# Quarter-array steps whose row halves add into the same two banks, with a drain of TensorE between

## The chip, the cores and the metric

The kernel runs on one core of a Trainium2 chip. The metric is the device time of one execution in microseconds. A core has five engines that this text names as the profile does: PE (TensorE, the matmul array, with its weight loads listed apart as PEld), DVE (VectorE), ACT (ScalarE), POOL (GpSimd) and SP (SyncE, which here only issues transfers). Matmul results go to eight PSUM banks of 128 partitions by 512 float32; only PE writes them, DVE and ACT read them out.

## The reference

Sigmoid attention on 8 batches of 12 heads, then a token mixer whose mixing matrix is made from the data:

```python
scores = q @ k.T / sqrt(64) - log(448)         # per batch and head, 448 x 448
x = (sigmoid(scores) @ v)                      # heads side by side: 8 x 448 x 768
wq, wk = x @ w_q, x @ w_k                      # 8 x 448 x 64 each
mixed = (wq @ wk.T / sqrt(64)) @ x             # 8 x 448 x 768
out = relu(mixed) @ w_out                      # 8 x 448 x 768, float32
```

The kernel computes `mixed` as `wq @ (wk.T @ x)`.

## The kernel before

**Units.** There are 24 quads: quad n = 3u + j holds four heads of batch u (j = 0, 1, 2). A head's 448 tokens are 7 blocks of 64. Everything on PE is bf16, and most of it runs in quarters of the array: a matmul of 64 rows by 64 columns of weights. Four such matmuls, one for each pair of row half and column half, run side by side; this text calls them a group. The column half decides which 64 partitions of a bank are written. The two row halves hold different parts of a sum or different operands, and they write different banks, so most steps take a pair of banks.

**Steps.** The order of the work is written out by hand in the string `PLAN`, one letter for each step; all engines' queues follow from it, and each engine works strictly in that order. The letters that matter here:

- S: scores of one block, four matmuls of 448 columns into a pair of banks, then one sigmoid on ACT (L303), which writes bf16. There are 168.
- P: sigmoid times v for one block, four matmuls of 448 columns, summed over seven steps; then the result `xt` is copied out of the banks by DVE (L329), or in halves by DVE and ACT (L327, letter R).
- x: transposes of `xt` to `xn`.
- W: `x @ [w_q w_k]` of batch u in six steps c = 0 to 5, one for each 128 columns of x. For u = 4, 5, 6 (letters L and l) the steps are tiled in quarters, step c takes `xt` of quad c // 2, and the two row halves sum into a bank each (L383). After step 5 one bank is copied to `wpart` (L390), the other is added to that on DVE (L391) and makes `wqk`; POOL copies half of it to `wq2` (L392).
- N: `wk` is transposed.
- U: `wk.T @ x` of batch u, here called `tmp`. For u = 3, 5, 6, 7 (letters T and t) it is tiled the same way, with 14 matmuls of 384 columns (L439), a copy of one bank to `upart` (L443) and an addition (L444).
- M: `wq @ tmp` with its relu (L448 on ACT, L450 on DVE), three steps for each batch.
- O: the output product. Batches 2 to 5 use whole sums per bank (`out_pair`, L509). Of the last two batches, three chunks of 128 tokens (letters I and i, `out_halves`, L549) are tiled in quarters: four parts, two for each block of 64 tokens. After the second part of a block, one bank is copied to the output tile `o` (L554) and the other added to it on DVE (L555). The other chunks run on the whole array, in halves of 384 output columns (`out_chunk`, L590, copies L614). The very last half is summed in one bank, and DVE copies 192 of its columns and ACT the other 192 (L611, L612).

**Banks.** The string `BANKS` lists by hand which bank or pair each step takes, in order of `PLAN`. A step's first matmul waits for the last reader of the bank.

**Loads.** SP issues the loads of q, k, v in the order of `ORDER`, at most eight tiles ahead of the casts to bf16. The two weights w_q and w_k are two transfers into one tile (L624); POOL casts that tile in four pieces (L720). v is cast to a tile ordered by block, then head pair (L202).

**The end.** After the last S come, in `PLAN`, the rest of batches 6 and 7: `x`, W of batch 7 on the whole array, N, U, M, twelve I steps, and sixteen O steps.

Of the kernel before, what the change touches and what calls it, by code (L numbers as in the profile page):

```python
# [17 lines left out]
def kernel(  # L18
# [29 lines left out]
    def pool(name, bufs, **kw):  # L48
# [30 lines left out]
    )  # L79
# [45 lines left out]
    def xt(u, j):  # L125
# [61 lines left out]
    def cast1(n, nm, e):  # L187
        if KIND[n] in "cer" and nm != "v":
            if n not in pq:
                pq[n] = p_c16.tile([P, 2, 2, NI, 32, 2], BF16, tag="qk16", name="qk16")  # L190
            f = pq[n]
            COPY[e](  # L192
                out=f[:, :, "qk".index(nm)].rearrange("p e i d y -> p e y i d"),
                in_=ld.pop((nm, n)).rearrange("p (y i e d) -> p e y i d", y=2, i=NI, e=2),
            )
            ld[nm + "16", n] = f
            if ("q16", n) in ld and ("k16", n) in ld:
                arrange(n, nc.gpsimd)
            return
        p = p_v16 if nm == "v" else p_c16  # L200
        t16 = p.tile([P, NI, 2, HD], BF16, tag=nm + "16", name=nm + "16")
# [111 lines left out]
    def values(n, i, tail, eng):  # L313
# [4 lines left out]
        for h in range(2):  # L318
            for g in range(2):
                nc.tensor.matmul(  # L320
                    ps[HALF[g], h, 0:S], ld["v16", n][HALF[h], i, g, :],
                    ats[n, i][HALF[h], g, :], start=(i == 0), stop=(i == NI - 1),
                )
# [52 lines left out]
    def mlp_wqk(u, c, tail, act, tiled):  # L376
        if c == 0:
            pw[u] = bank2() if tiled else bank1()
        fb, ps, _ = pw[u]
        if tiled:  # L380
            for y in range(2):
                for x in range(2):
                    nc.tensor.matmul(  # L383
                        ps[HALF[x], y, 0:S], wqk16[HALF[y], c, 64 * x : 64 * x + 64],
                        xt(u, c // 2)[HALF[y], c % 2, 0:S], start=(c == 0), stop=(c == NC - 1),
                    )
            if c == NC - 1:
                w, w2 = wqks[u % 2], wq2s[u % 2]
                part = p_one.tile([P, S], F32, tag="wpart", name="wpart")
                read(fb, COPY["s" if act else "v"](out=part, in_=ps[:, 0, 0:S]))  # L390
                read(fb, nc.vector.tensor_tensor(out=w[:, 0:S], in0=ps[:, 1, 0:S], in1=part, op=ALU.add))  # L391
                nc.gpsimd.tensor_copy(out=w2[HALF[1]], in_=w[HALF[0], 0:S])  # L392
            return
# [4 lines left out]
        if c == NC - 1:  # L398
            w, w2 = wqks[u % 2], wq2s[u % 2]
            read(fb, nc.vector.tensor_copy(out=w[:, 0:S], in_=ps))  # L400
# [29 lines left out]
    def mlp_tmp_tiled(u, act):  # L430
        tmps[u] = p_one.tile([P, NB], BF16, tag="tmp", name="tmp")
        part = p_one.tile([P, NB], F32, tag="upart", name="upart")
        fb, ps, _ = bank2()
        for m in range(4):
            for r in range(2):
                if 2 * m + r == NI:
                    continue
                for y in range(2):
                    nc.tensor.matmul(  # L439
                        ps[HALF[y], r, 0:NB], wkn[u][HALF[r], m, :], xns[u][HALF[r], m, y * NB : (y + 1) * NB],  # L440
                        start=(m == 0), stop=(m == 3 - r),
                    )
        read(fb, COPY["s" if act else "v"](out=part, in_=ps[:, 0, 0:NB]))  # L443
        read(fb, nc.vector.tensor_tensor(out=tmps[u], in0=ps[:, 1, 0:NB], in1=part, op=ALU.add))  # L444

# [85 lines left out]

    def out_halves(act):

        if opened:
            w, m, part, fb, ps = opened.pop()
        else:
            w, m, nb = chunks.pop(0)
            assert nb < 0
            part = 0
            ot[0] = p_o.tile([P, 2, NB], F32, tag="o", name="o")  # L540
        o = ot[0]
        b, h = divmod(part, 2)
        if not h:
            fb, ps, _ = bank2()
        for c in range(3 * h, 3 * h + 3):
            t0 = 2 * S * c + m * P + b * NP
            for y in range(2):
                for x in range(2):
                    nc.tensor.matmul(  # L549
                        ps[HALF[x], y, 0:NB], mxs[w][HALF[y], t0 : t0 + NP], wout16[HALF[y], c, x * NB : (x + 1) * NB],  # L550
                        start=(c == 0), stop=(c == NC - 1),
                    )
        if h:
            read(fb, COPY["s" if act else "v"](out=o[:, b], in_=ps[:, 0, 0:NB]), keep=True)  # L554
            read(fb, nc.vector.tensor_tensor(out=o[:, b], in0=ps[:, 1, 0:NB], in1=o[:, b], op=ALU.add), keep=True)  # L555
        if part < 3:
            opened.append((w, m, part + 1, fb, ps))
            return
        (b0, i0), (b1, i1) = divmod(2 * m, NI), divmod(2 * m + 1, NI)
        for x in range(2):  # L560
# [11 lines left out]
    def out_chunk(act, tail):  # L572
# [22 lines left out]
        def store(cols):  # L595
            for y in range(2):
# [5 lines left out]
                )  # L602

        ps = ps[:, 0:NB] if not part else ps
# [4 lines left out]
        if w == NU // 2 - 1 and not chunks:  # L609
            h = NB // 2  # L610
            read(fb, nc.vector.tensor_copy(out=o[:, NB : NB + h], in_=ps[:, 0:h]), keep=True)  # L611
            read(fb, nc.scalar.copy(out=o[:, NB + h :], in_=ps[:, h:]), keep=True)  # L612
        else:
            read(fb, COPY["s" if act else "v"](out=o[:, nb * NB : (nb + 1) * NB], in_=ps), keep=True)  # L614
        split = tail and w == NU // 2 - 1 and m == NI - 1
# [5 lines left out]
    def load_weights():  # L621
        w32["qk"] = p_ld.tile([P, 2 * NI * HD], F32, tag="ld", name="w32")[:, 0:D]
        for x, w in enumerate((moe_w_q, moe_w_k)):
            nc.sync.dma_start(  # L624
                out=w32["qk"].rearrange("p (c n) -> p c n", c=NC)[:, :, 64 * x : 64 * x + 64],
                in_=w.rearrange("(c p) n -> p c n", p=P)
            )

# [48 lines left out]
    OTHERS = set(BY["s"] + BY["v"])  # L677
    ORDER = [(x[0], int(x[1:])) for x in ORDER.replace(".", "").lower().split()]
    done = dict.fromkeys("SPqkKxWNUMOCgz", 0)
# [4 lines left out]
    def pump_loads():  # L684
        while len(loaded) < len(ORDER):
            nm, n = ORDER[len(loaded)]
            if nm == "w" and n:
                loaded.add((nm, n))
# [22 lines left out]
    def cast_now(nm, n, e):  # L711
# [5 lines left out]
        else:  # L717
            for h in range(2):
                for g in range(2):
                    COPY[e](  # L720
                        out=wqk16[HALF[g], h::2],
                        in_=w32["qk"].rearrange("p (c n) -> p c n", c=NC)[HALF[h], g::2],
                    )
        cast.add((nm, n))
# [4 lines left out]
    def pump():  # L729
        while pumped[0] < len(ORDER):  # L730
            nm, n = ORDER[pumped[0]]
            if (nm, n) not in OTHERS:
                if not ready(nm, n):
                    break
                cast_now(nm, n, "g")
            pumped[0] += 1
# [31 lines left out]

    ALIKE = dict(a="q", c="q", e="q", r="q", b="k", d="k", f="k", s="k", j="k", h="k", X="x", y="x", Y="x", g="g", z="z", L="W", l="W", T="U", t="U", I="O", i="O", Q="O", G="M", R="P")
    done["q"] = done["k"] = 1  # L770
    quads_r = []

    for t in PLAN:
# [59 lines left out]
        elif kind == "O":  # L833
            if (opened or chunks)[0][0] in TW:
                out_pair(t == "o", t == "Q")
            elif t in "Ii":
                out_halves(t == "i")
            else:
# [30 lines left out]
```

## Time and profile before

| | us |
|---|---|
| timed runs | 182.22, 183.09, 185.05 (median 183.09) |
| the profiled execution | 182.05 |
| its span, first to last instruction | 180.3 |
| PE busy from 160 to 180 | 16.11 |
| ACT busy from 160 to 180 | 7.18 |

The span is what the profile shows; the execution's own time adds what lies around it. In the profile, a line such as `L298 PE MATMUL banks<-qk 64*64 64x448 bf16 x672` is a group of alike instructions: line 298 of the kernel, the engine, what it writes and reads, the part of the array (64*64 is a quarter), partitions by columns, and the count. A time line gives start, length, engine and line, and in brackets how long the engine had been idle before and what released it. Matmuls overlap: a quarter matmul of 448 columns is listed with some 0.35 us, while groups of four follow each other every 0.19 us.

### The profile page before, as it was taken

The page shows a single profiled execution, that of the slowest core. Times are in us where ns is not written, and L with a number is a line of the kernel's source. Part 1 is how long each engine was busy: PE and PEld are TensorE (multiplying, and loading weights), DVE is VectorE, ACT ScalarE, POOL GpSimd, SP SyncE. Part 2 cuts the span into 40 slices and gives each one's busy share as a digit, 9 for nine tenths or more (in the row PEclk, how much of TensorE's full clock was granted, in tenths as well). Part 3 has the DMA queues.
Part 4 walks back from the last instruction along what each step waited for, and adds up shares of the span by engine and source line. Part 5 has one row for each costly group of instructions (what it writes and reads, how often), then busy time and mean ns, then how long its engine had stood idle before and what let it go on. Part 6 is the DMA issues. An engine that isn't in the chain of part 4 may idle for free.

```text
span 180.3 us, 7970 instructions
## 1 busy us (share of the span) xinstructions
PE 169.6 (94%) x3471; PEld 112.5 (62%) x3472; DVE 142.1 (79%) x229; ACT 160.0 (89%) x212; POOL 123.4 (68%) x168
## 2 busy tenths in 40 slices
PE   7787899889999999999999999999999999999990
PEld 7333555554455445655686768778987789778560
DVE  3239599998989899889899879887999866588810
ACT  4699999999999999999999989999999899985240
POOL 1397799998998999999999999989306990000000
PEclk9999999999999999999999999999999999999998
DMA  5999999999999799989998999983946744442686
GB/s 174 356 394 387 331 382 376 288 302 364 411 340 346 181 306 292 372 285 288 313 282 285 281 374 346 316 266 96 264 118 155 226 95 107 91 91 46 157 241 175
DMA packets 24915, 47.31 MB, mean 262 GB/s; under 512 B 3888, under 2 KB 18480, under 8 KB 24880
## 3 DMA queue, kind: packets, MB, share of 16 engines
q1 hardware_dynamic: 23680, 44.84, 77.0%
q0 software_dynamic: 800, 1.18, 3.6%
q10 hardware_dynamic: 400, 0.79, 1.4%
q8 instruction: 27, 0.44, 1.0%
q14 instruction: 8, 0.07, 0.1%
HBM read 35.78 MB, written 11.01 MB: 260 GB/s over the span
## 4 chain that ended last, share of the span: by engine, by line
PE 67%; DVE 14%; DMA 9%; POOL 4%; SPq 2%; ACT 2%; issue 2%
PE banks L298 13%; PE banks L320 13%; PE banks L590 13%; PE banks L509 11%; DVE qk L232 4%; DMA k<-in_k_dram 4%; DMA v<-in_v_dram 3%; PE banks L549 3%; PE banks L395 3%; DVE xt L329 3%; POOL qk L192 3%; PE banks L358 2%; DVE qk L256 2%; DVE xn L347 1%; DMA out_dram<-o 1%
## 5 line engine op out<-in xcount | busy, mean ns | idle before, releaser
L303 ACT ACTIVATE at<-banks 128x896 bf16<-128x896 f32 x168 | 140.9, 946 | 3.6 <-PE banks L298 2.7
L298 PE MATMUL banks<-qk 64*64 64x448 bf16 x672 | 62.5, 357 | 2.5 <-DVE xt L329 1.4
L320 PE MATMUL banks<-at,v 64*64 64x448 bf16 x672 | 46.5, 350 | 0.1
L298 PEld LDWEIGHTS <-qk 64*64 64x64 bf16 x672 | 25.8, 105 | 21.1 <-issue 12.5
L509 PE MATMUL banks<-wout,mx 64*64 64x384 bf16 x672 | 36.3, 323 | 0.0
L320 PEld LDWEIGHTS <-v 64*64 64x64 bf16 x672 | 23.7, 106 | 6.9 <-issue 0.8
L509 PEld LDWEIGHTS <-mx 64*64 64x64 bf16 x672 | 23.3, 107 | 4.3
L590 PE MATMUL banks<-wout,mx 128*128 128x384 bf16 x132 | 24.8, 327 | 0.0
L192 POOL CAST qk<-q 128x896 bf16<-128x896 f32 x19 | 22.6, 1191 | 0.7 <-DMA q<-in_q_dram 0.2
L450 DVE TENSOR_SCALAR mx<-banks 128x512 bf16<-128x512 f32 (+3 forms) x24 | 21.0, 882 | 2.4 <-PE banks L477 1.6
L161 POOL COPY swap<-qk 32x448 uint32<-32x448 uint32 x28 | 15.8, 564 | 10.2 <-DVE qk L192 8.5
L192 POOL CAST qk<-k 128x896 bf16<-128x896 f32 x18 | 21.5, 1194 | 1.8 <-POOL qk L167 0.9
L329 DVE CAST xt<-banks 128x896 bf16<-128x896 f32 x19 | 20.5, 1081 | 1.4 <-PE banks L320 1.0
L202 POOL CAST v<-v 128x896 bf16<-128x896 f32 x20 | 18.4, 931 | 0.6
L590 PEld LDWEIGHTS <-mx 128*128 128x128 bf16 x132 | 11.9, 98 | 10.7 <-issue 3.9
L164 POOL COPY qk<-qk 32x448 uint32<-32x448 uint32 x28 | 16.6, 592 | 1.6
L263 DVE STREAM_TRANSPOSE qk<-qk 128x448 f32<-128x448 f32 x28 | 17.3, 630 | 0.1
L167 POOL COPY qk<-swap 32x448 uint32<-32x448 uint32 x28 | 15.8, 564 | 1.6
L232 DVE STREAM_TRANSPOSE qk<-qk 32x448 f32<-32x448 f32 x24 | 15.3, 636 | 0.6
L371 DVE COPY xn<-banks 128x1024 bf16<-128x1024 bf16 (+1 forms) x17 | 11.1, 654 | 4.6 <-PE banks L358 4.6
L614 DVE COPY o<-banks 128x384 f32<-128x384 f32 x15 | 8.2, 550 | 1.6 <-PE banks L590 0.8
L358 PEld LDWEIGHTS <-xt 64*64 64x64 bf16 x544 | 7.6, 109 | 1.9 <-issue 1.0
(87 smaller groups left out, 196.2 us busy)
## 6 DMA issues: line engine op xcount, KB each, us to landing
q<-in_q_dram SPq DMA_DIRECT2D x24, 448.0 KB, 7.0
v<-in_v_dram SPq DMA_DIRECT2D x24, 448.0 KB, 6.3
k<-in_k_dram SPq DMA_DIRECT2D x23, 448.0 KB, 7.3
out_dram<-o SPq DMA_DIRECT2D x51, 192.0 KB, 3.5
wout<-in_moe_w_out_dram POOLq DMA_DIRECT2D x2, 576.0 KB, 12.1
wout<-wout SPq DMA_DIRECT2D x12, 96.0 KB, 5.2
out_dram<-o ACTq DMA_DIRECT2D x3, 192.0 KB, 3.4
k<-in_k_dram SPq DMA_DIRECT2D x1, 256.0 KB, 5.2
```

Of the source, the lines that this page charges most:

```text
L164: eng.tensor_copy(out=w[hi, 0], in_=w[lo, 1])
L192: COPY[e](out=f[:, :, "qk".index(nm)].rearrange("p e i d y -> p e y i d"), in_=ld.pop((nm, n)).rearrange("p (y i e d) -> p e y i d", y=2, ...
L202: COPY[e](out=t16.rearrange("p i b d -> p b i d"), in_=ld.pop((nm, n)).rearrange("p b (i d) -> p b i d", i=NI),)
L232: nc.vector.transpose(out=qk[n][other : other + 32, h].rearrange("p t i n -> p (t i n)").bitcast(F32), in_=w[own : own + 32, 1 - h],)
L263: nc.vector.transpose(out=qk[n][:, t].rearrange("p t i n -> p (t i n)").bitcast(F32), in_=w)
L298: nc.tensor.matmul(sc[HALF[h], g, 0:S], qk[n][HALF[g], h, 1, i, :], qk[n][HALF[g], h, 0].rearrange("p i n -> p (i n)"), start=True, stop=True,
L303: inst = nc.scalar.activation(at, sc[:, :, 0:S], ACTF.Sigmoid, bias=attn_bias, scale=attn_scale)
L320: nc.tensor.matmul(ps[HALF[g], h, 0:S], ld["v16", n][HALF[h], i, g, :], ats[n, i][HALF[h], g, :], start=(i == 0), stop=(i == NI - 1),)
L329: read(fb, COPY[eng](out=xt(u, j)[:, :, 0:S], in_=ps[:, :, 0:S]))
L450: inst = nc.vector.tensor_scalar(dst, ps, moe_scale, 0.0, ALU.mult, ALU.max)
L509: nc.tensor.matmul(ps[HALF[x], y, 0:NB], mx[HALF[y], u, b, 64 * (i - 3 * y) : 64 * (i - 3 * y) + 64], wout16[HALF[y], slot(y, b), x * NB : ...
L590: nc.tensor.matmul(ps, mxs[w][:, 2 * S * c + m * P : 2 * S * c + (m + 1) * P], wout16[:, c, w0:w1], start=(c == 0), stop=(c == NC - 1),)
```

## The change

In the tiled W, U and I steps both row halves now add into the same two banks. The columns (for I, the two token blocks) are split in two, one half for each bank. In a first pass row half 0 writes bank 0 and row half 1 bank 1; then PE is drained (`nc.tensor.drain()`); in a second pass the row halves change banks and add to what the other has left. At the end each bank holds a full sum, and one copy of both banks replaces the copy and the addition.

- W: six steps remain, with eight matmuls of 224 columns each. Step c takes both halves of quad c % 3 in pass c // 3; the drain stands ahead of step 3.
- U: 28 matmuls of 192 columns, with one drain in the middle.
- I: four parts of a chunk of 12 matmuls of 384 columns as before, with a drain ahead of part 2; one pair of banks for the chunk instead of two, and one copy of 768 columns after part 3, on DVE (I) or ACT (i). The output tile is taken only there.
- The last output half: the two 192-column halves become separate sums in separate banks, each copied after its own six matmuls, the first by DVE, the second by ACT.
- `BANKS` is changed from batch 3 on, mostly by renaming; the letters of the last steps in `PLAN` change where the copies go.
- v is cast in one piece to a tile ordered by head pair, then block. The weights come in eight transfers (2 weights, 2 partition halves, 2 parities), and are cast in one piece.

The code also gets a way to cast v by transfer (`CASTING`, marked by a star in `ORDER`) and a letter J for split copies; no star stands in `ORDER` and no J in `PLAN`.

```diff
-        "wwwwyINIIItIiIGMiIMiIIOOOOOOOQOoOQOQOQ"
+        "wwwwyINIIItIIIGMiIMIIIOOOOOOOQOoOQOQOQ"
...
+        if nm == "v":
+            t16 = p_v16.tile([P, 2, NI, HD], BF16, tag="v16", name="v16")
...
+                COPY[e](
+                    out=t16.rearrange("p b i d -> p (b i d)"), in_=ld.pop((nm, n)).rearrange("p b x -> p (b x)"),
+                )
...
         if tiled:
-            for y in range(2):
-                for x in range(2):
-                    nc.tensor.matmul(
-                        ps[HALF[x], y, 0:S], wqk16[HALF[y], c, 64 * x : 64 * x + 64],
-                        xt(u, c // 2)[HALF[y], c % 2, 0:S], start=(c == 0), stop=(c == NC - 1),
-                    )
+            z, j = divmod(c, NJ)
+            if c == NJ:
+                nc.tensor.drain()
+            for b in (2 * j, 2 * j + 1):
+                for y in range(2):
+                    for x in range(2):
+                        nc.tensor.matmul(
+                            ps[HALF[x], y ^ z, 0 : S // 2], wqk16[HALF[y], b, 64 * x : 64 * x + 64],
+                            xt(u, j)[HALF[y], b % 2, (y ^ z) * S // 2 : (y ^ z) * S // 2 + S // 2],
+                            start=(z == b == 0), stop=(z == 1 and b == NC - 1),
+                        )
             if c == NC - 1:
-                w, w2 = wqks[u % 2], wq2s[u % 2]
-                part = p_one.tile([P, S], F32, tag="wpart", name="wpart")
-                read(fb, COPY["s" if act else "v"](out=part, in_=ps[:, 0, 0:S]))
-                read(fb, nc.vector.tensor_tensor(out=w[:, 0:S], in0=ps[:, 1, 0:S], in1=part, op=ALU.add))
-                nc.gpsimd.tensor_copy(out=w2[HALF[1]], in_=w[HALF[0], 0:S])
+                src = ps[:, :, 0 : S // 2]
+                read(fb, nc.vector.tensor_copy(out=w[:, 0:S].rearrange("p (z s) -> p z s", z=2), in_=src))
...
-        read(fb, COPY["s" if act else "v"](out=part, in_=ps[:, 0, 0:NB]))
-        read(fb, nc.vector.tensor_tensor(out=tmps[u], in0=ps[:, 1, 0:NB], in1=part, op=ALU.add))
+        h = NB // 2
+        for t in range(2):
+            if t:
+                nc.tensor.drain()
+            for m in range(4):
+                for r in range(2):
+                    if 2 * m + r == NI:
+                        continue
+                    z = r ^ t
+                    for y in range(2):
+                        nc.tensor.matmul(
+                            ps[HALF[y], z, 0:h], wkn[u][HALF[r], m, :],
+                            xns[u][HALF[r], m, y * NB + z * h : y * NB + z * h + h],
+                            start=(t == m == 0), stop=(t == 1 and m == 3 - r),
+                        )
+        read(fb, COPY["s" if act else "v"](
+            out=tmps[u].rearrange("p (z x) -> p z x", z=2), in_=ps[:, :, 0:h],
+        ))
...
-    def out_halves(act):
+    def out_halves(act, split):
...
+        z, h = divmod(part, 2)
+        if part == 2:
+            nc.tensor.drain()
         for c in range(3 * h, 3 * h + 3):
             for y in range(2):
+                t0 = 2 * S * c + m * P + (y ^ z) * NP
                 for x in range(2):
                     nc.tensor.matmul(
-                        ps[HALF[x], y, 0:NB], mxs[w][HALF[y], t0 : t0 + NP], wout16[HALF[y], c, x * NB : (x + 1) * NB],
-                        start=(c == 0), stop=(c == NC - 1),
+                        ps[HALF[x], y ^ z, 0:NB], mxs[w][HALF[y], t0 : t0 + NP],
+                        wout16[HALF[y], c, x * NB : (x + 1) * NB],
+                        start=(part == 0 and c == 0), stop=(z == 1 and c == NC - 1),
                     )
-        if h:
-            read(fb, COPY["s" if act else "v"](out=o[:, b], in_=ps[:, 0, 0:NB]), keep=True)
-            read(fb, nc.vector.tensor_tensor(out=o[:, b], in0=ps[:, 1, 0:NB], in1=o[:, b], op=ALU.add), keep=True)
...
+            read(fb, COPY["s" if act else "v"](out=o, in_=ps[:, :, 0:NB]), keep=True)
...
+        if nb and w == NU // 2 - 1 and not chunks:
+            if part:
+                fb, ps, _ = bank1()
+            h = NB // 2
+            c0 = NB + part * h
+            block(ps[:, 0:h], c0, c0 + h, 0, NC)
+            read(fb, COPY["vs"[part]](out=o[:, c0 : c0 + h], in_=ps[:, 0:h]), keep=True)
...
-            nc.sync.dma_start(
-                out=w32["qk"].rearrange("p (c n) -> p c n", c=NC)[:, :, 64 * x : 64 * x + 64],
-                in_=w.rearrange("(c p) n -> p c n", p=P)
-            )
+            for g in range(2):
+                for h in range(2):
+                    nc.sync.dma_start(
+                        out=w32["qk"][HALF[g]].rearrange("p (j h n) -> p h j n", j=NJ, h=2)[:, h, :, 64 * x : 64 * x + 64],
+                        in_=w.rearrange("(j g h d) n -> g h d j n", j=NJ, g=2, h=2)[g, h],
+                    )
...
-            for h in range(2):
-                for g in range(2):
-                    COPY[e](
-                        out=wqk16[HALF[g], h::2],
-                        in_=w32["qk"].rearrange("p (c n) -> p c n", c=NC)[HALF[h], g::2],
-                    )
+            COPY[e](out=wqk16.rearrange("p c n -> p (c n)"), in_=w32["qk"])
```

More of the change, by code (lines that the diff above doesn't have):

```diff
@@ L199, in cast1 @@
             return
-        p = p_v16 if nm == "v" else p_c16
-        t16 = p.tile([P, NI, 2, HD], BF16, tag=nm + "16", name=nm + "16")
+        if nm == "v":
+            t16 = p_v16.tile([P, 2, NI, HD], BF16, tag="v16", name="v16")
+            if e == "d":
+                u, j = quads[n]
+                nc.gpsimd.dma_start(
+                    out=t16.rearrange("p b i d -> p b (i d)"),
+                    in_=v[u, 4 * j : 4 * j + 4].rearrange("(g h) (p i) d -> (h p) g (i d)", g=2, i=NI),
+                )
+            else:
+                COPY[e](
+                    out=t16.rearrange("p b i d -> p (b i d)"), in_=ld.pop((nm, n)).rearrange("p b x -> p (b x)"),
+                )
+            ld["v16", n] = t16
+            return
+        t16 = p_c16.tile([P, NI, 2, HD], BF16, tag=nm + "16", name=nm + "16")
         COPY[e](
@@ L379, in mlp_wqk @@
         fb, ps, _ = pw[u]
+        w, w2 = wqks[u % 2], wq2s[u % 2]
         if tiled:
-            for y in range(2):
-                for x in range(2):
-                    nc.tensor.matmul(
-                        ps[HALF[x], y, 0:S], wqk16[HALF[y], c, 64 * x : 64 * x + 64],
-                        xt(u, c // 2)[HALF[y], c % 2, 0:S], start=(c == 0), stop=(c == NC - 1),
-                    )
-            if c == NC - 1:
-                w, w2 = wqks[u % 2], wq2s[u % 2]
-                part = p_one.tile([P, S], F32, tag="wpart", name="wpart")
-                read(fb, COPY["s" if act else "v"](out=part, in_=ps[:, 0, 0:S]))
-                read(fb, nc.vector.tensor_tensor(out=w[:, 0:S], in0=ps[:, 1, 0:S], in1=part, op=ALU.add))
-                nc.gpsimd.tensor_copy(out=w2[HALF[1]], in_=w[HALF[0], 0:S])
+            z, j = divmod(c, NJ)
[9 more added lines that the diff above has]
+                        )
+            if c == NC - 1:
+                src = ps[:, :, 0 : S // 2]
+                read(fb, nc.vector.tensor_copy(out=w[:, 0:S].rearrange("p (z s) -> p z s", z=2), in_=src))
+                if tail or act:
+                    read(fb, nc.scalar.copy(out=w2[HALF[1]].rearrange("p (z s) -> p z s", z=2), in_=src[HALF[0]]))
+                else:
+                    nc.gpsimd.tensor_copy(out=w2[HALF[1]], in_=w[HALF[0], 0:S])
             return
@@ L431, in mlp_tmp_tiled @@
         tmps[u] = p_one.tile([P, NB], BF16, tag="tmp", name="tmp")
-        part = p_one.tile([P, NB], F32, tag="upart", name="upart")
         fb, ps, _ = bank2()
[L434 to L441, printed above, removed]
-                    )
-        read(fb, COPY["s" if act else "v"](out=part, in_=ps[:, 0, 0:NB]))
-        read(fb, nc.vector.tensor_tensor(out=tmps[u], in0=ps[:, 1, 0:NB], in1=part, op=ALU.add))
+        h = NB // 2
[16 more added lines that the diff above has]
+        ))
     def relu(fb, dst, ps, act):
@@ L558, in out_halves @@
             return
+        o = p_o.tile([P, 2, NB], F32, tag="o", name="o")
+        if split:
+            for b in range(2):
+                read(fb, COPY["vs"[b]](out=o[:, b], in_=ps[:, b, 0:NB]), keep=True)
+        else:
+            read(fb, COPY["s" if act else "v"](out=o, in_=ps[:, :, 0:NB]), keep=True)
         (b0, i0), (b1, i1) = divmod(2 * m, NI), divmod(2 * m + 1, NI)
@@ L602, in store @@
                 )
+        if nb and w == NU // 2 - 1 and not chunks:
[5 more added lines that the diff above has]
+            read(fb, COPY["vs"[part]](out=o[:, c0 : c0 + h], in_=ps[:, 0:h]), keep=True)
+            if part:
+                store(slice(NB, D))
+            else:
+                opened.append((w, m, nb, fb, ps))
+            return
         ps = ps[:, 0:NB] if not part else ps
@@ L608, in out_chunk @@
             return
[L609 to L614, printed above, removed]
+        read(fb, COPY["s" if act else "v"](out=o[:, nb * NB : (nb + 1) * NB], in_=ps), keep=True)
         split = tail and w == NU // 2 - 1 and m == NI - 1
@@ L677 @@
     OTHERS = set(BY["s"] + BY["v"])
-    ORDER = [(x[0], int(x[1:])) for x in ORDER.replace(".", "").lower().split()]
+    CASTING = {("v", int(x[2:])) for x in ORDER.split() if x[0] == "*"}
+    ORDER = [(x[0], int(x[1:])) for x in ORDER.replace(".", "").replace("*", "").lower().split()]
     done = dict.fromkeys("SPqkKxWNUMOCgz", 0)
@@ L686, in pump_loads @@
             nm, n = ORDER[len(loaded)]
-            if nm == "w" and n:
+            if nm == "w" and n or (nm, n) in CASTING:
                 loaded.add((nm, n))
@@ L835 @@
                 out_pair(t == "o", t == "Q")
-            elif t in "Ii":
-                out_halves(t == "i")
+            elif t in "IiJ":
+                out_halves(t == "i", t == "J")
             else:
```

14 lines of the change are left out of this document (4 added, 10 removed), and 16 rows, old and new, of the table BANKS.

## The prediction

> **What bounds the kernel now.** I read the page's shares first, then the chain of waits, the busy time by stretches, and the groups of one stretch.
>
> ```profile
> PE 169.6 (94%) x3471; PEld 112.5 (62%) x3472; DVE 142.1 (79%) x229; ACT 160.0 (89%) x212; POOL 123.4 (68%) x168
> ...
> PE 67%; DVE 14%; DMA 9%; POOL 4%; SPq 2%; ACT 2%; issue 2%
> ```
> ```profile
> 100.00:120.00 20.00, 19.60 (x476) 14.92 (x469) 17.13 (x28) 19.36 (x27) 18.25 (x26) 1.00 0.96 328
> 120.00:140.00 20.00, 19.92 (x557) 16.47 (x553) 17.93 (x29) 19.72 (x29) 10.65 (x16) 1.00 0.60 168
> 140.00:160.00 20.00, 20.00 (x550) 16.41 (x539) 13.81 (x23) 19.17 (x28) 8.33 (x12) 1.00 0.50 122
> ```
>
> The columns of a stretch are PE, weight loads, DVE, ACT and POOL. PE and ACT are both nearly full, DVE is not. A busy PE proves little, because matmuls overlap and a gap under a matmul's length hides, so I rebuild 120 to 140 us from the pace of groups of four quarter matmuls, which run side by side:
>
> ```profile
> L509 PE MATMUL banks<-wout,mx 64*64 64x384 bf16 x232 | 12.7, 323 | 0.0
> L298 PE MATMUL banks<-qk 64*64 64x448 bf16 x75 | 7.4, 354 | 0.1
> L320 PE MATMUL banks<-at,v 64*64 64x448 bf16 x84 | 5.6, 350 | 0.0
> ```
> ```profile
> 123.84 0.49 PE banks L509 x12
> 124.33 0.22 PE banks L463 x8
> ...
> 135.88 1.14 PE banks L320 x24
> ```
>
> The chain gives 0.49/3 = 0.163 us per group at 384 columns, 0.22/2 = 0.11 at 256 and 1.14/6 = 0.19 at 448. The three big rows make 58 x 0.163 + (18.75 + 21) x 0.19 = 17.0 us; the smaller rows of that view (40 matmuls at 256 columns, 14 at 384, 8 at 448, 104 transposes at 0.034 a group, from the row at 160.50 below) add 2.9. That is 19.9 of 20 us: PE streams without a gap, the clock column says 1.00, and whatever makes PE stand still there is paid in full. VectorE, which the change relieves, has 2 us of idle time in that stretch.
>
> **Drains: ten of them.** One falls in each tiled W (u = 4, 5, 6), in each tiled U (u = 3, 5, 6, 7) and in each of three half-output chunks at the end. No drain stands inside the old stream, so I bound its cost. From below: PE empties by itself when the tiling changes from quarters to the whole array.
>
> ```profile
> 108.96 0.68 PE L509 MATMUL banks<-wout,mx 64*64 64x384 bf16 x12
> 109.57 0.61 PE L342 MATMUL banks<-ident,xt 128*128 128x128 bf16 x8
> ```
> ```profile
> 159.26 1.31 PE L395 MATMUL banks<-xt,wqk 128*128 128x448 bf16 x6
> 160.60 0.62 DVE L400 CAST wqk<-banks 128x448 bf16<-128x448 f32 x1
> ```
> ```profile
> 142.99 0.62 DVE L391 TENSOR_TENSOR wqk<-banks,wpart 128x448 bf16<-128x448 f32 x1
> 143.67 0.37 PEld L410 LDWEIGHTS <-wqk 64*64 64x64 bf16 x8 [0.16 <-DVE wqk L391]
> 143.72 0.42 PE L410 MATMUL banks<-ident,wqk 64*64 64x64 bf16 x7
> ```
>
> Three groups from 108.96 stream until 109.45; the next matmul starts at 109.57: 0.12 us. From above: a matmul's last result. Six matmuls from 159.26 at 0.19 stream until 160.40 and the reader starts at 160.60, 0.20 later. Then a restart with nothing loaded: release at 143.61, matmul at 143.72, 0.11. Together 0.31; one hop between engines is in both, so I take 0.27. The end of the program has a real drain of PE's sequencer:
>
> ```profile
> L864 PEldq DRAIN x2: 13/1564/3115, 173.0 to 179.8; - x2
> ```
> ```profile
> 168.14 7.97 PE L590 MATMUL banks<-wout,mx 128*128 128x384 bf16 x48
> ```
>
> It starts at 173.0, lasts 3.115 and ends at 176.1, just where the last matmul ends (168.14 + 7.97). So a drain costs no fixed microsecond, but it takes away a lead of 3 us over the array. Refilling that is not shown anywhere; I allow up to 0.5 a drain. Ten at 0.27 are **+2.70** (1.2 to 5.0).
>
> The Trainium skill, page "TensorE: Matmul & The Clock Gate", section "Single matmul latency", has a constant of 166 ns besides the columns; by it alone the drains would be about 1.7, an estimate between my bounds.
>
> **Short matmuls.** W goes from 24 matmuls of 448 columns to 48 of 224, three times; U from 14 of 384 to 28 of 192, four times; the last output half from 6 of 384 to 12 of 192. The columns streamed are the same, and cost more only where a group has a floor.
>
> ```profile
> 160.50 0.45 PE L358 MATMUL banks<-ident,xt 64*64 64x64 bf16 x32
> 160.77 0.66 PE L549 MATMUL banks<-wout,mx 64*64 64x384 bf16 x12
> ```
>
> Eight groups of 64 columns pass in 0.27 us, 0.034 each, far under the 0.08 that 192 columns need, and 256 columns ran at 0.11, in proportion. For the last half, eight matmuls of 128 columns took 0.61 with their tail (109.57 above). **0.00**, at most +0.3.
>
> **W asks for its inputs earlier.** Step c used xt of quad c // 2; now steps 0, 1, 2 use quads 0, 1, 2. For u = 4 and u = 6 the third xt is long there. For u = 5 it isn't:
>
> ```profile
> 118.70 0.76 PE L383 MATMUL banks<-xt,wqk 64*64 64x448 bf16 x12
> 118.76 0.61 DVE L327 CAST xt<-banks 128x448 bf16<-128x448 f32 x1
> ...
> 119.46 0.39 PE L383 MATMUL banks<-xt,wqk 64*64 64x448 bf16 x4
> ```
>
> Steps 1 to 3 start at 118.70; step 2 would come at 118.89, but its xt is ready at 119.37 and PE at about 119.42. Behind it queue W3 to W5 and two score steps, which feed ACT. Before, step 4 at 119.46 just missed that wait. **+0.53** (0.3 to 0.7).
>
> **What comes back.** PE had one wait that lies after these steps, for a buffer that DVE empties:
>
> ```profile
> 122.70 0.67 PE L509 MATMUL banks<-wout,mx 64*64 64x384 bf16 x12
> ...
> 122.85 0.56 DVE L520 COPY o<-banks 128x384 f32<-128x384 f32 x1 [1.16 <-DMA v<-in_v_dram]
> ...
> 123.46 0.38 PE L298 MATMUL banks<-qk 64*64 64x448 bf16 x4
> ```
>
> Three groups from 122.70 end at 123.19, PE goes on at 123.46: a later PE loses **-0.27** of its delay here, since DVE waited for a transfer. The additions themselves:
>
> ```profile
> L390 DVE COPY wpart<-banks 128x448 f32<-128x448 f32 x3 | 1.8, 612 | 0.0
> L444 DVE TENSOR_TENSOR tmp<-banks,upart 128x384 bf16<-128x384 f32 x4 | 2.2, 555 | 0.1
> L554 DVE COPY o<-banks 128x384 f32<-128x384 f32 x3 | 1.7, 551 | 0.2 <-PE banks L549 0.2
> L522 DVE COPY o<-banks 128x768 f32<-128x768 f32 x6 | 5.7, 956 | 2.8 <-ACT at L303 1.9 <-issue 0.4 <-PE banks L509 0.4
> ```
>
> Each W and U loses one operation (0.612 and 0.555); each output chunk has one copy of 768 columns (0.956) for two pairs (2.2). That is 1.8 + 2.2 + 3.8 = 7.8 us of DVE and ACT, most of it beside PE. PE waited for it in two places: 0.16 for u = 6 (143.67 above, **-0.16**) and once in the tail. The last copies shorten as well:
>
> ```profile
> 165.01 0.14 PEld L477 LDWEIGHTS <-tmp 64*64 64x64 bf16 x8 [0.31 <-DVE tmp L444]
> ...
> 176.15 0.36 DVE L611 COPY o<-banks 128x192 f32<-128x192 f32 x1 [4.05 <-PE banks L590]
> 176.54 0.32 ACT L612 COPY o<-banks 128x192 f32<-128x192 f32 x1 [0.69 <-DVE o L611]
> ```
>
> The new U copies once on ACT while three output parts run on PE: **-0.31**. At the end ACT copied its half only after DVE, on one bank; now DVE's half is copied beside the second half's matmuls, and 176.54 - 176.15 = **-0.39** goes.
>
> **Loads and casts at nothing.** The weights come in eight transfers instead of two, on SP, ahead of k5, q5 and the loads after them:
>
> ```profile
> 13.14 0.38 SPq L624 DMA_DIRECT2D w<-in_moe_w_q_dram  x1
> 13.57 1.31 SPq L624 DMA_DIRECT2D w<-in_moe_w_k_dram  x1
> 14.98 2.08 SPq L173 DMA_DIRECT2D k<-in_k_dram  x1
> ```
> ```profile
> 12.00:26.00 14.00, 11.86 (x233) 6.62 (x232) 11.11 (x16) 14.00 (x19) 11.91 (x14) 1.00 1.08 367
> ```
> ```profile
> L720 POOL CAST wqk<-w x4: 500/503/506, 22.0 to 23.7; 64x384 bf16<-64x384 f32 x4
> ```
>
> Six issues more at 0.38 are 2.3 us of SP. The cover: the 16 transfer engines are full there (share 1.08), and SP's issues already stretch to 1.3 and 2.1 us. Without it the next loads come up to 2.3 late. POOL gets back some of it, one cast for four of 0.503. The v cast only changes its order of writing. **0.00**, between -0.3 and +2.
>
> **Sum.** 2.70 + 0.53 - 0.27 - 0.16 - 0.31 - 0.39 = +2.10 us. The profiled execution took 182.05 (span 180.3), so 184.15. The three timed runs have a median of 183.09, 1.04 above it; on that scale I forecast **185.2 us**, 1.1% slower.
>
> **Rivals.** *Dear drains* (18%): the lost lead has to be refilled. Nothing speaks against it but the dense transposes, which were queued before they ran. At 0.5 a drain the sum is 2.3 us more, 187.5. *Cheap drains* (15%): 0.12 as at a change of tiling, 1.5 less, 183.7; against it, a sequencer that drains can't load weights ahead. *A floor per matmul* (4%): if a weight load and its matmul can't pass faster than in the output steps (0.163/4 = 0.041), 224 columns cost 0.163 a group instead of 0.095: 12 groups x 0.068 x 3 = 2.4, and 8 x 0.081 x 4 = 2.6 for U, in all 190.2. The transposes speak against it, at 0.034 for four. The Trainium skill, "TensorEngine Tiling (Array Packing)", section "Instruction Overhead", speaks for it: some 60 cycles each, and a tiling factor shouldn't be taken from a dimension that is already small. *Late loads* (7%): 1 to 2 us more, about 186.7. *Faster, on the other side* (5%): DVE and ACT, which empty the banks, set the pace, and PE only looks full. The place is the stretch from 88 to 150 us, where 3 x 0.612 + 3 x 0.555 = 3.5 us of emptying go; if all came back, and the drains lay in PE's waiting, 3.5 + 0.31 + 0.39 are 4.2 less, 178.9. It decides once a score step waits longer for a free bank than a drain lasts; the 19.9 of 20 us and VectorE's 2 idle us speak against it. That leaves 51% for the forecast.
>
> **Range and chances.** Cheap drains give 183.7, and a fast run of them lies up to 1 us lower; dear ones reach 187.5, with late loads 188.5. So 182.6 to 188.5. Two per cent of 183.09 are 3.7 us, about what a measurement of this kernel can tell from no change: slower than 186.8 are dear drains, the floor, and half of late loads with a little of the forecast's edge, 0.29; faster than 179.4 only the last rival, 0.05; within, 0.66.
>
> **What would show it.** After each drain, PE's next weight load starts about 0.2 us past the last column, and 0.5 or more for dear drains. W's third step of u = 5 starts when DVE's xt ends. No wait stands before L477's successor in the tail, and ACT's last copy follows PE directly. If the stretches from 120 us show PE streaming less than 19.5 of 20 without ending later, or scores waiting for banks, I was wrong on the bound; if k5 and q5 land over 2 us later and ACT stands idle near 30 us, on the loads.

## The result and the profile after

| | before | after |
|---|---|---|
| median of 4 runs, us | 182.86 (182.22 to 185.05) | 189.28 (188.88 to 190.83) |
| profiled execution: span, us | 180.3 | 187.8 |

The ratio is 1.0379, with a 95% interval from 1.0298 to 1.046: slower by 6.4 us, where 2.1 were forecast. The time lies above the forecast range of 182.6 to 188.5. Some executions of a kernel fall into a slower state; the ratios here and below leave these out, the medians don't.

The page of the changed kernel, its first and its fourth part (busy shares; the chain of waits by engine and by line):

```profile
PE 172.7 (92%) x3606; PEld 114.0 (61%) x3606; DVE 136.9 (73%) x215; ACT 160.3 (85%) x210; POOL 122.5 (65%) x165
...
PE 40%; POOL 25%; DMA 20%; DVE 5%; issue 3%; ACT 2%; SPq 2%; ACTq 0%; POOLq 0%
PE banks L538 13%; DMA k<-in_k_dram 12%; POOL qk L192 10%; PE banks L333 7%; PE banks L311 6%; DMA v<-in_v_dram 5%; POOL v L209 4%; POOL swap L161 4%; POOL qk L164 4%; POOL qk L167 4%; PE banks L578 3%; PE banks L623 2%; DMA wout<-wout 2%; PE banks L371 2%; DMA out_dram<-o 1%
```

DVE is busy 5 us less, as meant. But the chain changed its nature: PE's share fell from 67% to 40%, and POOL and transfers hold 45%, where they had 13%. A longer stop of PE can't do that; something earlier holds back the loads. The busy time by stretches, columns as before with the clock, the transfer engines' share and GB/s last, shows where, first of the kernel before, then of the changed one:

```profile
18.00:20.00 2.00, 1.37 (x29) 0.81 (x32) 0.80 (x2) 2.00 (x4) 2.00 (x2) 1.00 1.25 273
20.00:22.00 2.00, 2.00 (x88) 1.43 (x87) 1.38 (x2) 2.00 (x4) 1.06 (x2) 1.00 1.05 371
22.00:24.00 2.00, 1.95 (x43) 1.16 (x36) 1.97 (x4) 2.00 (x3) 1.83 (x4) 1.00 1.07 391
```
```profile
18.00:20.00 2.00, 1.34 (x25) 0.78 (x28) 0.83 (x2) 2.00 (x4) 1.36 (x2) 1.00 0.81 155
20.00:22.00 2.00, 1.80 (x84) 1.31 (x87) 1.35 (x2) 2.00 (x4) 1.74 (x2) 1.00 0.36 81
22.00:24.00 2.00, 1.95 (x44) 1.16 (x39) 1.97 (x3) 2.00 (x4) 0.39 (x1) 1.00 0.47 82
```

For four microseconds the transfers run at 81 to 82 GB/s where they ran at 371 to 391; this text calls such a stretch a hole. SP's and POOL's queues in time, of the changed kernel, say what was issued then and who waited:

```profile
13.17 3.43 SPq L667 DMA_DIRECT2D w<-in_moe_w_q_dram  x4
17.20 4.82 SPq L667 DMA_DIRECT2D w<-in_moe_w_k_dram  x4
22.11 0.66 SPq L173 DMA_DIRECT2D k<-in_k_dram  x1
```
```profile
24.10 0.83 POOL L762 CAST wqk<-w 128x768 bf16<-128x768 f32 x1 [1.71 <-DMA w<-in_moe_w_k_dram]
26.28 1.19 POOL L192 CAST qk<-k 128x896 bf16<-128x896 f32 x1 [1.36 <-DMA k<-in_k_dram]
...
38.46 1.20 POOL L192 CAST qk<-k 128x896 bf16<-128x896 f32 x1 [0.99 <-DMA k<-in_k_dram]
```

The eight weight transfers hold SP from 13.2 to 22.0, and the next load of k, issued at 14.98 before, goes out at 22.11. POOL casts it at 26.28 instead of 24.25, and a later k at 38.46 instead of 34.36. From there POOL, whose casts feed everything, stays some 4.5 us late to 113 us.

### The profile page after: what moved, and what is told of

Read it like the earlier page. It is cut to its first block, busy times and chain, and to the rows that moved or that the text cites. A ratio compares the mean times of both kernels' runs of the same rounds, so it can differ in the third digit from the quotient of the medians.

```text
span 187.8 us, 8239 instructions
## 1 busy us (share of the span) xinstructions
PE 172.7 (92%) x3606; PEld 114.0 (61%) x3606; DVE 136.9 (73%) x215; ACT 160.3 (85%) x210; POOL 122.5 (65%) x165
## 4 chain that ended last, share of the span: by engine, by line
PE 40%; POOL 25%; DMA 20%; DVE 5%; issue 3%; ACT 2%; SPq 2%; ACTq 0%; POOLq 0%
PE banks L538 13%; DMA k<-in_k_dram 12%; POOL qk L192 10%; PE banks L333 7%; PE banks L311 6%; DMA v<-in_v_dram 5%; POOL v L209 4%; POOL swap L161 4%; POOL qk L164 4%; POOL qk L167 4%; PE banks L578 3%; PE banks L623 2%; DMA wout<-wout 2%; PE banks L371 2%; DMA out_dram<-o 1%
## 5 line engine op out<-in xcount | busy, mean ns | idle before, releaser
L311 PE MATMUL banks<-qk 64*64 64x448 bf16 x672 | 61.7, 357 | 2.1 <-ACT at L316 1.1
L311 PEld LDWEIGHTS <-qk 64*64 64x64 bf16 x672 | 25.1, 105 | 19.9 <-issue 12.0
L623 PE MATMUL banks<-wout,mx 128*128 128x384 bf16 (+1 forms) x138 | 24.8, 320 | 0.4 <-DVE xn L384 0.4
L623 PEld LDWEIGHTS <-mx 128*128 128x128 bf16 x138 | 12.4, 98 | 10.8 <-issue 4.3
L477 ACT ACTIVATE mx<-banks 128x512 bf16<-128x512 f32 (+1 forms) x13 | 7.5, 592 | 2.1 <-PE banks L506 1.5
```

The costliest lines, as they stand in the source:

```text
L311: nc.tensor.matmul(sc[HALF[h], g, 0:S], qk[n][HALF[g], h, 1, i, :], qk[n][HALF[g], h, 0].rearrange("p i n -> p (i n)"), start=True, stop=True,
L623: nc.tensor.matmul(ps, mxs[w][:, 2 * S * c + m * P : 2 * S * c + (m + 1) * P], wout16[:, c, w0:w1], start=(c == 0), stop=(c == NC - 1),)
```

## The experiments

Each was timed beside the kernel before; ratios are to that.

**Which part costs it: loads or drains.** The first two runs put back and put in the weight load alone (each with its cast), the third puts in the drains alone.

```diff
 e1_two_transfers (on the changed kernel)
+            nc.sync.dma_start(
+                out=w32["qk"].rearrange("p (c n) -> p c n", c=NC)[:, :, 64 * x : 64 * x + 64],
+                in_=w.rearrange("(c p) n -> p c n", p=P)
+            )
 e2_eight_transfers (on the kernel before)
+            for g in range(2):
+                for h in range(2):
+                    nc.sync.dma_start(
...
 e3_drains_alone (on the kernel before; the same in U at m == 2, in a chunk at part == 2)
+            if c == NJ:
+                nc.tensor.drain()
```

> The changed kernel with one part undone: the two weights come in two transfers of 192 KB again and are cast in four pieces. Theory L (the eight small transfers starve the loads behind them; the trace shows the transfer rate at 81 GB/s from 20 to 24 us where it was 371 to 391): most of the loss goes, about 185, some 1.2% over the kernel before. Theory D (drains and quarter matmuls cost far more than the 0.25 us each that the trace shows): still about 189, ratio 1.035.

> The kernel before with only the weight load and its cast changed to eight transfers of 48 KB and one cast. Theory L: 3 to 4.5 us slower than before, about 186.5, with the same hole in the transfer rate near 20 us. Theory D: no slower than 0.5 us, about 183.

> The kernel before with ten drains put where the change has them (ahead of step 3 of each tiled W, in the middle of each tiled U, ahead of part 2 of each half-output chunk), nothing else changed. Theory L with drains at 0.25 us: at most 2.5 us slower, about 185. Theory D: 5 us or more, about 188.

Measured: with two transfers 185.79 us, ratio 1.0174 (1.0115 to 1.0233); eight transfers alone 186.81, ratio 1.0216 (1.0167 to 1.0265); drains alone 185.37, ratio 1.0147 (1.009 to 1.0204). The parts add up: 1.0174 + 0.0216 is 1.039, the change has 1.0379. So the transfers make over half of the loss, 3.5 to 3.7 us, and the drains most of the rest. With two transfers the chain is PE's again and the rate is back (part 4 of the page; the stretch from 20 to 24 us):

```profile
PE 72%; DVE 14%; DMA 4%; ACT 2%; issue 2%; POOL 1%; SPq 1%; ACTq 1%
```
```profile
20.00:22.00 2.00, 1.81 (x50) 1.20 (x40) 1.80 (x3) 2.00 (x3) 1.58 (x2) 1.00 1.06 362
22.00:24.00 2.00, 1.95 (x40) 1.20 (x36) 1.97 (x3) 2.00 (x4) 1.34 (x3) 1.00 1.02 359
```

**Why eight transfers starve the loads.** The trace has an issue time and a landing time for each SP transfer. Set beside the landing of the eighth transfer before it, the issues of the changed kernel read (us):

```
transfer      issued   8th before it landed   itself landed
w_q, third     14.64   14.31                  22.05
w_q, fourth    15.99   15.55                  22.25
w_k, first     17.20   17.18                  22.45
w_k, second    18.41   18.40                  22.66
w_k, third     19.98   19.96                  23.56
w_k, fourth    21.42   21.40                  23.78
```

The last four go out 0.01 to 0.02 us after that landing, and the view of SP's waits counts 2.9 us of them ahead of the weight transfers (in all, how often, the longest):

```profile
SPq L667 <- DMA v<-in_v_dram: 1.4, 2, 0.8
SPq L667 <- DMA k<-in_k_dram: 0.9, 1, 0.9
SPq L667 <- DMA q<-in_q_dram: 0.6, 1, 0.6
```

So SP has at most eight transfers under way; this text says that each holds one of eight places. The trace's own records tell where the eight comes from. SP's transfers use eight semaphores in turn (numbers 101 and 104 to 110; a transfer raises its semaphore when it has landed), and each of them waits for the one that it is about to use, that is, for the eighth transfer before it. The eight is thus written into this program; no run shows a limit of the queue itself.

The eight weight transfers of 48 KB landed between 21.63 and 23.78, behind the last load issued ahead of them (21.40), and so 2.4 to 8.5 us after their issue. One can therefore hold its place as long as a load of 448 KB (7.2 us for v, the median from 12 to 26 us). Three runs test that. In the first the eight are kept but in two clumps of four; in the second and third, tiny transfers that nothing reads are added to the kernel before, behind its weights and, ten of them, behind v5, where SP was idle.

```diff
 e4_two_clumps (on the changed kernel; w8 is the second weight, in a tile of its own)
+        "... v1 w0 q4 k4 v2 w8 k5 q5 ..."
 e5_six_tiny (on the kernel before, behind the weights)
+        for y in range(6):
+            nc.sync.dma_start(out=tiny[0:64, y : y + 1], in_=moe_w_q[0:64, y : y + 1])
 e9_ten_tiny_later (on the kernel before)
+            if (nm, n) == ("v", 5):
+                for y in range(10):
+                    nc.sync.dma_start(out=tiny[0:64, y : y + 1], in_=moe_w_q[0:64, y : y + 1])
```

> The changed kernel with the eight weight transfers kept, but in two clumps of four, into a tile each, the first ahead of q4 and the second where all eight were; two casts. If at most eight SP loads can be under way at once (each new one starts only after the landing of the eighth before it), four small ones leave four large loads of 448 KB in flight, the hole shrinks and most of the loss from loads goes: 185 to 187. If it is SP's own time for issuing eight transfers, that stays the same: about 189.

Measured: 189.63 us, ratio 1.0381 (1.0305 to 1.0458). No gain; the expectation failed, and the time is the one that was expected of SP's own time. Two clumps take eight places between them, as one does, and the transfer rate drops twice: to 286 and 306 GB/s from 14 to 18 us, where the kernel before had 396 and 385, and to 121 and 109 from 20 to 24. SP's queue from 8 us:

```profile
8.74 3.02 SPq L667 DMA_DIRECT2D w<-in_moe_w_q_dram  x4
12.42 0.35 SPq L173 DMA_DIRECT2D q<-in_q_dram  x1
13.61 0.34 SPq L173 DMA_DIRECT2D k<-in_k_dram  x1
16.58 0.38 SPq L179 DMA_DIRECT2D v<-in_v_dram  x1
17.96 2.57 SPq L667 DMA_DIRECT2D w<-in_moe_w_k_dram  x4
```

This run alone can't tell places from SP's own time: in the second clump the transfers followed each other every 0.65 us, while the landings of the eighth before had come 0.3 us and more earlier. The loads between the clumps did go out on such landings (k at 13.61 on 13.55, v at 16.58 on 16.52). Why the two clumps cost as much as one was not tried further.

> The kernel before, its two weight transfers kept, with six transfers of 64 x 4 bytes added behind them on SP (nothing reads them). They bring as many transfers as the change does, but no bytes. Theory W (eight places: each SP load starts only when the eighth before it has landed, so small transfers crowd out large ones): the next load of k comes at about 22 us instead of 15, the hole is there, 2.5 to 4 us slower, about 186. Theory P (the 256-byte pieces of 64 partitions are what is slow): no slower than 0.5 us, about 183.5.

Measured: 187.33 us, ratio 1.0244 (1.019 to 1.0297). Six transfers of 256 bytes each cost as much as eight of 48 KB, so it takes neither the bytes nor pieces of 256 bytes. SP's queue, and the rate from 20 us:

```profile
14.30 6.73 SPq L630 DMA_DIRECT2D tiny<-in_moe_w_q_dram  x6
21.13 1.08 SPq L173 DMA_DIRECT2D k<-in_k_dram  x1
```
```profile
20.00:22.00 2.00, 1.76 (x36) 1.08 (x35) 1.97 (x3) 2.00 (x4) 1.58 (x3) 1.00 0.18 23
```

This run doesn't tell places from SP's own time either. SP was issuing all the while (2.91 and 1.21 us for the first two, 0.60 for each of the others), and every landing that a tiny transfer had to await had come before.

> The kernel before with ten transfers of 64 x 4 bytes on SP behind the load of v5, where SP stands idle for some 2.6 us (21.6 to 24.2) and the loads under way last until 30.3. Theory W (eight places on SP): the ninth and tenth wait for the first two, which land only behind v5, so the load of q after them is issued at about 31 us instead of 24.2, the transfer rate falls to a few GB/s for 2 to 3 us near 31, and the kernel is 1.5 to 4 us slower. Theory T (SP's own time, ten times 0.4 to 0.6 us, is what delays the loads): the load of q is issued by 27.5, the loads under way cover that, no hole, no slower than 0.5 us.

Measured: 188.64 us, ratio 1.0348 (1.0266 to 1.0429), more than expected. Where SP had time to spare, ten tiny transfers took it from 22.11 to 32.45, the load of q came at 32.55 instead of 24.21, and POOL stood still for it:

```profile
22.11 10.34 SPq L700 DMA_DIRECT2D tiny<-in_moe_w_q_dram  x10
32.55 0.53 SPq L173 DMA_DIRECT2D q<-in_q_dram  x1
```
```profile
39.13 1.20 POOL L192 CAST qk<-q 128x896 bf16<-128x896 f32 x1 [5.70 <-DMA q<-in_q_dram]
```

The issues again follow the landings of the eighth before: 23.25 on 23.23, 24.41 on 24.39, 25.59 on 25.58, 28.01 on 27.99, 30.38 on 30.36. The ten issues themselves add up to 5.4 us (0.47 each for most, 0.93 at most); the other 5.0 are waits for landings:

```profile
SPq L700 <- DMA v<-in_v_dram: 2.1, 3, 0.7
SPq L700 <- DMA q<-in_q_dram: 1.4, 2, 0.7
SPq L700 <- DMA k<-in_k_dram: 1.3, 2, 0.8
SPq L700 <- DMA w<-in_moe_w_k_dram: 0.2, 1, 0.2
```

By SP's own time alone the load of q would have gone out by 28; that it went out at 32.55 is due to the eight places.

The loss is 6.0 us by the medians, and clock may explain a part of what came on top of the expected 4. In this run's profile PE stood still from 43.3 to 47.1 us, and its granted clock was 0.69 from 46 to 48 us and 0.50 from 48 to 50. The profiles of the eight transfers alone and of the two clumps show 0.50 behind a stop of PE, too; those of the changed kernel and of the six tiny transfers show 1.00 behind theirs. This was not tried apart.

**What a drain is made of.**

```diff
 e8_drains_twice (on the kernel before with the ten drains)
-                nc.tensor.drain()
+                nc.tensor.drain(), nc.tensor.drain()
```

> The kernel before with each of the ten drains put twice in a row. If a drain costs only the emptying of the array, the second finds it empty and adds under 0.05 us each: as with one, ratio 1.015, and 0.44 us from the last old group to the first new one. If each drain costs a fixed time of its own: twice the loss, ratio 1.03.

Measured: 186.51 us, ratio 1.0221 (1.017 to 1.0272), between the two expectations. The source view of W's drains, three pairs, and the trace's times for one pair:

```profile
L382 PEldq DRAIN  x6: 13/300/915, 107.6 to 142.9; - x6
```
```
kernel          last group starts   drain ends   next load   next group   from group to group
drains alone    108.12              108.50       108.55      108.56       0.44
drains twice    107.82              108.19, 108.27   108.33  108.33       0.51
```

The second drain lasts 13 ns and moves the next group by 0.07 us, a little more than the 0.05 that emptying alone was to allow. So a drain is nearly all emptying and starting again; its own handling is small, and the ratio's interval overlaps that of single drains.

**The early need of W at u = 5.**

```diff
 e7_u5_old_sum (on the changed kernel with two transfers)
-        if tiled:
+        if tiled and u == 5:
+            (the four matmuls of 448 columns, the copy and the addition of the kernel before)
+        if tiled:
```

> The changed kernel with two weight transfers, and W of batch u = 5 summed in two banks and added as before (no drain and no early need for the third quad there). By the trace, 0.53 us of waiting and 0.25 us of a drain go: about 185.0 beside 185.8 with all three W's changed. If the wait is taken up elsewhere anyway: 185.8.

Measured: 184.65 us, ratio 1.0115 (1.0074 to 1.0155): 1.1 us less than with all three, where 0.78 were expected. The two intervals overlap, so the times alone don't show a gain; the wait itself stands in the changed kernel's timeline, below.

**The last copies.**

```diff
 e6_last_half_sp (on the kernel before, with the change's last output half)
-                eng = nc.scalar if tail and y else nc.sync
+                last = w == NU // 2 - 1 and m == NI - 1
+                eng = nc.scalar if tail and y and (not last or cols.start) else nc.sync
```

> The kernel before with only the last output half in two sums of 192 columns, and the stores of the half before it both on SP, so that ACT is free for its last copy. If the last copies are what ends the kernel: ACT's copy starts 0.05 us after PE's end and 0.35 to 0.4 us go, ratio 0.998. If the last transfers wait for something else: no change, ratio 1.000.

Measured: 182.45 us, ratio 1.0004 (0.9971 to 1.0037): no change. ACT's last copy came at 176.20 instead of 176.54, but SP now had four stores to issue at the end, and finished later than with three (SP's queue from 174 us, this run first, then the kernel before):

```profile
174.74 3.02 SPq L600 DMA_DIRECT2D out_dram<-o  x4
```
```profile
174.71 2.65 SPq L599 DMA_DIRECT2D out_dram<-o  x3
```

The last issue ends at 177.76 instead of 177.36. What the copies gained, the stores gave back.

No version here beats the kernel before.

## Why the prediction was wrong, point by point

**What bounds the kernel: right, but not for all of it.** From 120 us on PE set the pace, and with the loads put back the chain is PE's again. The reading looked at the shares and at the late stretches; it took the early loads for covered. The sign that it named for being wrong there came: k5 landed at 26.14 us instead of 23.00, and ACT stood idle for 0.39 us at 31 and for 1.22 us at 45, where it didn't in the kernel before.

**"Loads and casts at nothing": this step failed.** It saw 2.3 us of SP time and named the cover, transfer engines that were full. The rival "late loads" had 7% and 1 to 2 us; alone the transfers cost 3.7 us. First, SP's time was mis-sized. The eight transfers held SP for 8.8 us, where the two had held it for 1.7: 5.7 are the issues, 0.60 to 1.31 us each and not 0.38, and 2.9 are the waits for landings. Second, the cover was made of the very loads that the weights displaced: eight places, of which the change filled all with 48 KB. Even with no time for issuing, the next load of k could not have gone out before 21.63, when the first weight transfer landed. In the kernel before, no issue of that stretch came right on such a landing (14.98 against 14.27, 17.14 against 15.44), so the limit didn't show there; the prediction took the cover for safe without asking what it was made of. What the issues and the places each cost in the changed kernel was not tried apart.

The Trainium skill, page "DMA: Bandwidth & Descriptors", section "Rules for kernel authors", says that many small transfers should be joined into one, and that under 64 KB one pays mostly overhead. These runs agree at 48 KB (3.7 us for eight) and below, though the price here was paid by the loads queued behind.

**Drains: right.** 0.27 us each was forecast, out of 0.31 less a hop between engines for which no row gave the size. In the changed kernel PE's sequencer leaves the drain at these times, and the groups stand (us):

```
           last group starts   drain ends   next group   from group to group   undrained pace
W, u = 4   110.85              111.14       111.20       0.35                  0.095
U, u = 5   133.86              134.14       134.20       0.34                  0.08
I, chunk 2 171.21              171.57       171.63       0.42                  0.163
```

Each lost 0.25 to 0.26 (0.24 to 0.26 over all ten), ten make 2.5; alone they were timed at 2.3 us by the medians and at 2.7 by the ratio. "Dear drains" is out: refilling the queue cost nothing that shows. Of the bounds, emptying plus restart was the right one, and the pause at a change of tiling (0.12) was half of it. By the 166 ns of the Trainium skill, page "TensorE: Matmul & The Clock Gate", section "Single matmul latency", ten drains would be 1.7 us, as the prediction estimated; that is too little here, the traces show 0.25 each.

**Short matmuls: right.** Groups of 224 columns followed each other every 0.095 us and groups of 192 every 0.08, in proportion to their columns; the rival's floor of 0.041 us per matmul is out for quarters of the array. The Trainium skill's overhead of some 60 cycles for each matmul, page "TensorEngine Tiling (Array Packing)", section "Instruction Overhead", doesn't show at these sizes either; no run has a group of under 64 columns.

**W's early need: right.** Step 1 of u = 5 starts two groups at 123.72, done by 123.91, and step 2 waits for DVE until 124.45: 0.54 us, 0.53 forecast. The timeline of PE in the changed kernel:

```profile
123.72 0.39 PE L403 MATMUL banks<-xt,wqk 64*64 64x224 bf16 x8
124.45 0.39 PE L403 MATMUL banks<-xt,wqk 64*64 64x224 bf16 x8 [0.33 <-DVE xt L340]
```

**What comes back: mostly not.** The -0.27 was right. In the run with two transfers the three groups of that place start at 124.53 and end at 125.02, and PE goes on at 125.05: 0.03 is left of the wait.

The -0.31 ahead of M and the -0.16 for u = 6 were mis-sized. Both took the idle time of the weight loads for that of PE. In the kernel before, the lines of PE around these two places are:

```profile
163.38 1.69 PE L549 MATMUL banks<-wout,mx 64*64 64x384 bf16 x36
165.01 0.38 PE L477 MATMUL banks<-wqk,tmp 64*64 64x448 bf16 x2
```
```profile
142.71 1.17 PE L509 MATMUL banks<-wout,mx 64*64 64x384 bf16 x24
143.72 0.42 PE L410 MATMUL banks<-ident,wqk 64*64 64x64 bf16 x7
```

Nine groups of 0.163 from 163.38 end at 164.85, and the next matmul came at 165.01, so only 0.16 was there to gain. Six groups from 142.71 end at 143.69, and the next came at 143.72: 0.03. With two transfers that 0.03 is gone, but of the 0.16 some 0.1 stayed: nine groups and a drain of 0.25 from 166.34 end at 168.06, and the next matmul starts at 168.16.

```profile
166.34 1.99 PE L578 MATMUL banks<-wout,mx 64*64 64x384 bf16 x36
168.16 0.36 PE L506 MATMUL banks<-wqk,tmp 64*64 64x448 bf16 x2
```

The -0.39 at the end was not there: ACT had a store to issue in its place, and issuing is done in the same order as the copies. ACT's queue in the changed kernel:

```profile
183.28 0.50 ACTq L632 DMA_DIRECT2D out_dram<-o  x1
183.82 0.32 ACT L644 COPY o<-banks 128x192 f32<-128x192 f32 x1 [0.57 <-PE banks L623]
```

PE ended at 183.52, ACT was free at 183.78. From PE's end to the end of the span it took 4.2 us in the kernel before (176.1 to 180.3) and 4.3 in the changed one. So of the 1.13 us forecast to come back, 0.24 + 0.06 + 0.03 = 0.33 did.

**The sum without the loads** was forecast as 2.1 us, 1.1% above the kernel before. With the terms as measured it is 2.5 for the drains and 0.54 for W, less 0.33, or 2.7 us. The run with two transfers is 2.7 us above the kernel before by the medians (185.79 and 183.08), 1.74% by the ratio (1.15 to 2.33). The agreement is closer than that interval can vouch for.

**The rival on the other side** (DVE and ACT set the pace) is out: in the run with two transfers the same 5 us of DVE work went (137.2 us busy instead of 142.1), and it was still slower than the kernel before.

## What to carry to other kernels

When a change splits a transfer, count how many transfers the program lets be under way at once, and not only its bytes and issue time: look up, for each issue, whether it follows the landing of a transfer a fixed number before it. If it does, every small transfer takes the room of a large one, and a queue that looks busy is no cover. And an addition taken off an engine that isn't the bound is worth at most the waits that it ends on the engine that is, read from the pace of that engine's matmuls and not from the idle time of its weight loads.

## What the runs showed of the hardware that was not expected

- In these kernels SP has at most eight transfers under way, because the program gives them eight semaphores in turn: where that limit holds an issue back, it comes 0.01 to 0.07 us after the landing of the eighth before. Six transfers of 256 bytes cost 4.3 us.
- A drain of PE in a full stream of quarter matmuls costs 0.24 to 0.26 us over the pace in the changed kernel, whatever the columns (192, 224 or 384); a second one behind it 0.07, of which its record shows 13 ns.
- Quarter matmuls keep pace with their columns down to 192: 0.08 us for four.
